# Scores against the block summaries: two 64-query tiles in one TensorE product

## The chip, the cores and the metric

The kernel runs on one core of one Trainium2 chip. The metric is the device time of one execution in microseconds; lower is better. Of the kernel before there are three timed runs, with a median of 678.67 us, and one profiled execution, whose trace all views here are taken from.

## What is computed

The reference is an attention whose output goes through one feed-forward layer. Each query sees the keys less than 16 positions away and, beside them, one summary of each block of 32 keys (the maximum of the block's keys, the mean of its values). Batch is 4, heads 8, sequence 768, head dimension 64; the feed-forward layer has width 512 and inner width 2048.

```python
k_sum = k.reshape(B, H, nb, block, D).max(axis=3)      # block 32, nb 24
v_sum = v.reshape(B, H, nb, block, D).mean(axis=3)
scores_l = scale * np.matmul(q, k.transpose(0, 1, 3, 2))
mask_l = np.abs(pos[:, None] - pos[None, :]) < window  # window 16
scores_s = scale * np.einsum('bhsd,bhnd->bhsn', q, k_sum) + np.log(block)
a = softmax(concatenate([where(mask_l, scores_l, -1e9), scores_s]))
x = matmul(a, concatenate([v, v_sum]))                 # heads side by side: 3072 x 512
h = x @ w_in
return (h * np.cos(h)) @ w_out
```

## The kernel before

**Groups.** The attention is cut into 32 groups: eight blocks of 384 queries (half a sequence each, `blk` 0 to 7) by four pairs of heads (`a`, `b`, `c`, `d`). A group holds six tiles of 64 queries for two heads. A tile of 64 queries needs a window of 96 keys (64 and 16 on either side) and the 24 summaries, so 120 scores a query and head.

**Scores.** The transposed queries of both heads lie in `qd` (128 partitions: head dimension of the first head, then of the second; 384 columns, one a query), the transposed keys in `kd` of the head pair, with the 24 summaries behind the keys from column `KW` on. The scores of head `hh` are built in one PSUM bank, `self.sp[hh]`: partitions 0 to 63 hold the even tile of a pair (`s` = 0), 64 to 127 the odd one (`s` = 1), and the pairs `c` = 0, 1, 2 lie behind one another, 96 window columns and 24 summary columns each. `scores` (L553 to L566) writes them with four products for each tile: for each head one against the tile's own 96 keys and one against the 24 summaries. Each contracts over 64 partitions (one head) and writes 64 partitions (one tile), so it uses a 64x64 quarter of TensorE's 128x128 array; head and half of the pair choose the quarter. Inputs are fp32, and each product stands in the trace as two passes, each a weight load and a matmul.

In the first eight groups (`masks`) a product with the identity (L549) has put the mask into the bank, and the score products add to it; in the other 24 VectorE adds the mask as it takes the scores out (`scale`, L573). Then follow maximum, subtraction, exponential, sum and normalization (VectorE, GpSimd, ScalarE), a transposition of the probabilities (L619, or in later groups through DRAM), the products with the values (`values`, L663) and a split of the result into a high and a low part.

**The feed-forward layer.** Weights and activations are split into high and low parts (fp32r), and each product is made of three. A step is one slice of 128 of the inner width for one block of 384 rows: `up` (L707, 12 products of 384 columns), cosine by ScalarE and VectorE (L717 to L732), a split again (L343, L349), `down` (L751, 9 products of 512 columns). There are 128 steps, so 1536 products on L707 and 1152 on L751.

**Order.** One list written out by hand (`ORDER`) gives the order in which every engine's instructions are issued; nothing is rescheduled. A token such as `d7.sc.2.5` is one call: here the scores of group d of block 7 into banks 2 and 5. The scores of all groups but the first eight stand between steps of the feed-forward layer, most directly between an `up` (L707) or `down` (L751) and the next.

The part that issues the score products, before:

```python
for t in range(U):                       # six tiles
    c, s = divmod(t, 2)
    for hh in range(2):
        for lo, n, key in ((0, W, k0), (W, NB, KW)):
            nc.tensor.matmul(out=self.sp[hh][s * QT : (s + 1) * QT, c, lo : lo + n], ...)
```

Of the kernel before, what the change touches and what calls it, by code (L numbers as in the profile page):

```python
# [176 lines left out]
def tile_kernel(  # L177
# [20 lines left out]
    nc = tc.nc  # L198

    B, H, S, D = q.shape  # L200
    NT, DM = out.shape
    DF = w_in.shape[1]
    P = 128
    QT = 64
    W = QT + 2 * WINDOW
    NB = S // BLOCK
    SQ = 32
    NK = W + NB
    NPAIR = H // 2
    TB = S // 2  # L210
    U = TB // QT
    NG = NPAIR
    QC = TB // P
# [69 lines left out]
    for hh in range(2):  # L283
        rows = mask[hh * QT : (hh + 1) * QT, :, 0:W]

        nc.gpsimd.affine_select(
            out=rows, in_=rows, pattern=[[0, QC + 1], [1, W]], compare_op=ALU.is_ge,
# [3 lines left out]
            out=rows, in_=rows, pattern=[[0, QC + 1], [-1, W]], compare_op=ALU.is_ge,  # L291
# [7 lines left out]
    KW = WINDOW + S + WINDOW  # L299
# [122 lines left out]
    class Group:  # L422
# [130 lines left out]
        def scores(self, *two):  # L553
            if not self.masks:
                self.score_banks(two)
            for t in range(U):
                c, s = divmod(t, 2)
                k0 = self.base + t * QT
                for hh in range(2):
                    rows = slice(hh * D, (hh + 1) * D)  # L560
                    for lo, n, key in ((0, W, k0), (W, NB, KW)):
                        nc.tensor.matmul(  # L562
                            out=self.sp[hh][s * QT : (s + 1) * QT, c, lo : lo + n],
                            lhsT=self.qd[rows, t * QT : (t + 1) * QT], rhs=self.kd[rows, key : key + n],
                            start=not self.masks, stop=not self.masks or (c == QC - 1 and lo == W),
                        )  # L566

        def scale(self, hh, eng):
            out = self.sc.rearrange("p (c h) n -> p c h n", h=2)[:, :, hh, :]
# [260 lines left out]
    class Summaries:  # L830
# [16 lines left out]
        def sum(self, eng):  # L847
# [24 lines left out]
            lo="low_part", dn="down", fe="fetch", ad="add", ta="take", st="store",  # L872
# [39 lines left out]
```

## Time and profile before

| | |
|---|---|
| timed runs | 677.88, 678.67, 681.73 us (median 678.67) |
| profiled execution | 679.78 us, of which the span from first to last instruction is 678.0 |
| TensorE busy (matmuls) | 641.4 us, 95% of the span |
| TensorE weight loads | 564.8 us (most beside matmuls) |
| VectorE, ScalarE, GpSimd busy | 391.1, 411.6, 295.4 us |
| score products (L562) | 768 products, 1536 passes, from 12.5 to 547.4 us |
| mean granted TensorE clock | 0.984 |

How to read it: in the profile PE is TensorE's matmuls, PEld its weight loads, DVE is VectorE, ACT ScalarE, POOL GpSimd, SP the queue that issues transfers. A line such as L562 is a line of the kernel before; `banks` is all of PSUM, `kd` keys, `qd` queries (in the first groups also in a buffer named `late`), `xh` and `xl` the parts of the layer's input, `gh` and `gl` those of the gate, `w` the weights. "64\*64" behind an operation is rows\*columns of the array in use, "64x96" partitions and columns of the operand. Matmul records end where a model of the pipeline puts their end, so consecutive ones overlap. A row of the table by stage is a stretch, its length, then busy time and instruction count of each engine.

### The profile page before, as it was taken

To read this page: it belongs to the slowest core of one execution; us is meant where nothing else is said; L and a number is where in the kernel's file an instruction comes from. 1 tells how busy PE (TensorE), PEld (TensorE's weight loads), DVE (VectorE), ACT (ScalarE), POOL (GpSimd) and SP (SyncE) were. 2 spreads that over 40 slices of the span, in tenths; PEclk is the share of its full clock that TensorE was granted. 3 is DMA by queue.
4 is the path that set the end of the run, shared out by engine and by line. 5 is a ranking of instruction groups with operands and counts; after the bars stand their busy time and mean duration, and the time that the engine had idled before them with its cause. 6 is when DMAs were issued, how large, how long until landed. Compare 5 with 4: busy or idle time off the path is not lost.

```text
span 678.0 us, 13401 instructions
## 1 busy us (share of the span) xinstructions
PE 641.4 (95%) x5180; PEld 564.8 (83%) x5180; DVE 391.1 (58%) x642; ACT 411.6 (61%) x720; POOL 295.4 (44%) x312
## 2 busy tenths in 40 slices
PE   6439989999999999999999999999999999999996
PEld 4327768888888888888898888898898889899895
DVE  3889799987553467426775764248484652232221
ACT  3557887758765467646765765447666565455443
POOL 3665778655432355333444554414353442122221
PEclk9959999999999999999999999999999999999999
DMA  9797924442322323434545453433253440001001
GB/s 221 212 252 195 321 83 159 149 110 59 87 51 54 88 78 112 117 89 95 111 123 129 118 166 95 94 53 89 75 148 90 107 124 29 23 0 47 1 0 47
DMA packets 158543, 71.17 MB, mean 105 GB/s; under 512 B 129552, under 2 KB 147344, under 8 KB 158480
## 3 DMA queue, kind: packets, MB, share of 16 engines
q1 hardware_dynamic: 158480, 70.32, 39.0%
q8 instruction: 41, 0.67, 0.4%
q14 instruction: 22, 0.18, 0.1%
HBM read 52.99 MB, written 14.94 MB: 100 GB/s over the span
## 4 chain that ended last, share of the span: by engine, by line
PE 86%; DMA 5%; DVE 3%; ACT 2%; SPq 2%; POOL 2%; issue 1%; POOLq 0%; ACTq 0%; DVEq 0%
PE banks L707 38%; PE banks L751 37%; PE banks L562 4%; DMA late<-in_moe_w_out_dram 4%; PE banks L663 4%; SPq L449 1%; PE banks L549 1%; PE banks L619 1%; POOL w L349 1%; DMA kn<-in_v_dram 1%; DVE banks L400 1%; DVE banks L392 1%; DVE stage L386 1%; PE banks L495 0%; PE banks L508 0%
## 5 line engine op out<-in xcount | busy, mean ns | idle before, releaser
L707 PE MATMUL banks<-xh,w 128*128 128x384 f32 x1024 | 281.9, 338 | 0.0
L751 PE MATMUL banks<-w,gh 128*128 128x512 f32 x768 | 242.6, 397 | 0.0
L349 POOL TENSOR_TENSOR gl<-t,gh 128x384 fp32r<-128x384 f32 x123 | 126.0, 1026 | 251.1 <-ACT gh L343 185.7
L707 PEld LDWEIGHTS banks<-xh,w 128*128 128x128 f32 x1024 | 186.9, 188 | 4.7 <-DVE xl L349 0.2
L707 PE MATMUL banks<-xl,w 128*128 128x384 f32 x512 | 171.8, 336 | 0.0
L751 PEld LDWEIGHTS banks<-w,gh 128*128 128x128 f32 x768 | 140.2, 188 | 25.6 <-ACT gh L343 0.2
L751 PE MATMUL banks<-w,gl 128*128 128x512 f32 x384 | 151.7, 395 | 0.6 <-POOL gl L349 0.4
L720 DVE SCALAR_TENSOR_TENSOR t<-t,banks 128x384 f32<-128x384 int32 x128 | 70.3, 549 | 127.6 <-ACT t L717 127.4
L717 ACT ACTIVATE t<-banks 128x384 int32<-128x384 f32 x128 | 62.4, 487 | 104.0 <-PE banks L707 100.3
L732 DVE SCALAR_TENSOR_TENSOR t<-t,banks 128x384 f32<-128x384 f32 x128 | 70.2, 549 | 75.5 <-ACT t L728 75.0
L707 PEld LDWEIGHTS banks<-xl,w 128*128 128x128 f32 x512 | 96.1, 188 | 3.8
L725 ACT ACTIVATE t<-t 128x384 f32<-128x384 f32 x128 | 67.2, 525 | 44.1 <-DVE t L720 43.8
L343 ACT CAST gh<-t 128x384 fp32r<-128x384 f32 x115 | 58.8, 512 | 55.1 <-DVE t L732 50.9
L751 PEld LDWEIGHTS banks<-w,gl 128*128 128x128 f32 x384 | 72.0, 188 | 18.0 <-POOL gl L349 2.4
L728 ACT ACTIVATE t<-t 128x384 f32<-128x384 f32 x128 | 67.2, 525 | 3.6
L586 POOL TENSOR_TENSOR sc<-sc,m 128x720 f32<-128x720 f32 x28 | 40.7, 1453 | 41.8 <-DVE m L581 39.0
L610 POOL TENSOR_TENSOR sc<-sc,r 128x720 f32<-128x720 f32 x28 | 38.9, 1392 | 38.5 <-DVE r L607 33.7
L349 POOL TENSOR_TENSOR w<-stage,w 128x1024 fp32r<-128x1024 f32 x15 | 36.6, 2440 | 18.2 <-ACT w L343 17.5
L562 PEld LDWEIGHTS banks<-kd,qd 64*64 64x64 f32 x1344 | 27.5, 132 | 7.9 <-issue 5.5
L602 DVE TENSOR_REDUCE r<-sc 128x6 f32<-128x726 f32 x28 | 25.2, 902 | 14.5 <-ACT sc L599 14.4
L725 ACT ACT_TABLE_LOAD x24 | 30.8, 1283 | 0.4
L562 PE MATMUL banks<-kd,qd 64*64 64x96 f32 (+1 forms) x1344 | 30.4, 231 | 0.1
(97 smaller groups left out, 577.4 us busy)
## 6 DMA issues: line engine op xcount, KB each, us to landing
late<-in_moe_w_in_dram SPq DMA_DIRECT2D x16, 512.0 KB
late<-in_moe_w_out_dram SPq DMA_DIRECT2D x16, 512.0 KB
pd<-stage SPq DMA_DIRECT2D x20, 384.0 KB
vn<-in_v_dram SPq DMA_DIRECT2D x52, 120.0 KB
out_dram<-stage SPq DMA_DIRECT2D x24, 256.0 KB
pt<-pd SPq DMA_DIRECT2D x60, 96.0 KB
kn<-in_v_dram SPq DMA_DIRECT2D x24, 192.0 KB
qn<-in_q_dram SPq DMA_DIRECT2D x80, 48.0 KB
```

The source lines that it names most:

```text
L343: eng.copy(out=out, in_=in_)
L349: eng.tensor_tensor(out=lo, in0=src, in1=hi.bitcast(F32), op=ALU.subtract)
L562: nc.tensor.matmul(out=self.sp[hh][s * QT : (s + 1) * QT, c, lo : lo + n], lhsT=self.qd[rows, t * QT : (t + 1) * QT], rhs=self.kd[rows, ke ...
L586: nc.gpsimd.tensor_tensor(out=self.sc, in0=self.sc, in1=self.m.unsqueeze(2).broadcast_to([P, U, NK]), op=ALU.subtract)
L610: nc.gpsimd.tensor_tensor(out=self.sc, in0=self.sc, in1=self.r.unsqueeze(2).broadcast_to([P, U, NK]), op=ALU.mult)
L707: nc.tensor.matmul(out=self.h, lhsT=w_of(name, self.f)[:, c * P : (c + 1) * P], rhs=x_of(self.blk, part, c), start=n == 0, stop=n == last,)
L717: nc.scalar.activation(out=self.t.bitcast(I32), in_=self.h, func=AF.Copy, scale=1.0 / TWO_PI)
L720: nc.vector.scalar_tensor_tensor(out=self.t, in0=self.t.bitcast(I32), scalar=-TWO_PI, in1=self.h, op0=ALU.mult, op1=ALU.add)
L725: nc.scalar.activation(out=self.t, in_=self.t, func=AF.Sin, scale=0.5)
L728: nc.scalar.activation(out=self.t, in_=self.t, func=AF.Square, scale=math.sqrt(2.0))
L732: nc.vector.scalar_tensor_tensor(out=self.t, in0=self.t, scalar=-1.0, in1=self.h, op0=ALU.add, op1=ALU.mult)
L751: nc.tensor.matmul(out=self.acc[i], lhsT=g[:, i * P : (i + 1) * P], rhs=w_of(name, self.f), start=self.first and n == 0, stop=self.last an ...
```

## The change

The products against the 24 summaries are the same for every query of a head, so two neighbouring tiles can share one. For each pair `c` the changed kernel first issues the four window products (two tiles by two heads, 64x64 each), and then for each head one product of all 128 queries of the pair with the summaries: it contracts over 64 partitions and writes 128, so it uses a 64x128 half of the array. A group has 12 + 6 = 18 products in place of 24. What is computed, where it is put, and the order of calls are the same.

```diff
-            for t in range(U):
-                c, s = divmod(t, 2)
-                k0 = self.base + t * QT
+            for c in range(QC):
+
+                for s, hh in itertools.product(range(2), range(2)):
+                    rows, k0 = slice(hh * D, (hh + 1) * D), self.base + (2 * c + s) * QT
+                    nc.tensor.matmul(
+                        out=self.sp[hh][s * QT : (s + 1) * QT, c, :W],
+                        lhsT=self.qd[rows, (2 * c + s) * QT : (2 * c + s + 1) * QT], rhs=self.kd[rows, k0 : k0 + W],
+                        start=not self.masks, stop=not self.masks,
+                    )
                 for hh in range(2):
                     rows = slice(hh * D, (hh + 1) * D)
-                    for lo, n, key in ((0, W, k0), (W, NB, KW)):
-                        nc.tensor.matmul(
-                            out=self.sp[hh][s * QT : (s + 1) * QT, c, lo : lo + n],
-                            lhsT=self.qd[rows, t * QT : (t + 1) * QT], rhs=self.kd[rows, key : key + n],
-                            start=not self.masks, stop=not self.masks or (c == QC - 1 and lo == W),
-                        )
+                    nc.tensor.matmul(
+                        out=self.sp[hh][:, c, W:NK],
+                        lhsT=self.qd[rows, c * P : (c + 1) * P], rhs=self.kd[rows, KW : KW + NB],
+                        start=not self.masks, stop=not self.masks or c == QC - 1,
+                    )
```

The order of instructions shows what this does on TensorE; rows that read alike one after the other are counted (x4). The first place is the last score group of the program, between a `down` (L751) and an `up`. Here is its beginning before, where `64x96` is a window product and `64x24` a summary product (partitions of the weights' columns written, by columns):

```order
L751 MATMUL banks<-w_394,gh 128x512 x2
L751 MATMUL banks<-w_394,gl 128x512
L562 MATMUL banks<-kd_102,qd 64x96
L562 MATMUL banks<-kd_102,qd 64x24
L562 MATMUL banks<-kd_102,qd 64x96
L562 MATMUL banks<-kd_102,qd 64x24
```

The last two rows go on in turn to 24 products. The same group whole in the changed kernel, where L561 is the window product, L568 the summary product, L757 `down` and L713 `up`:

```order
L757 MATMUL banks<-w_370,gl 128x512
L561 MATMUL banks<-kd_102,qd 64x96 x4
L568 MATMUL banks<-kd_102,qd 128x24 x2
L561 MATMUL banks<-kd_102,qd 64x96 x4
L568 MATMUL banks<-kd_102,qd 128x24 x2
L561 MATMUL banks<-kd_102,qd 64x96 x4
L568 MATMUL banks<-kd_102,qd 128x24 x2
L713 MATMUL banks<-xh_6_5151,w_680 128x384
```

Window and summary products no longer take turns one by one; they stand in six runs of four and two, and every second run writes 128 partitions.

The second place is in the start of the program, on TensorE as well, where the scores of the second block's first group follow the mask product (L549, after the change L550) and a product with the values (L663, L669). Before:

```order
L495 MATMUL banks<-ident,late_128 128x128 x3
L663 MATMUL banks<-pt,x_1_136 64x64 x12
L549 MATMUL banks<-mask,ident 128x360 x2
L562 MATMUL banks<-kd_99,qd 64x96
L562 MATMUL banks<-kd_99,qd 64x24
```

The changed kernel at the same place:

```order
L496 MATMUL banks<-ident,late_128 128x128 x3
L669 MATMUL banks<-pt,x_1_136 64x64 x12
L550 MATMUL banks<-mask,ident 128x360 x2
L561 MATMUL banks<-kd_99,qd 64x96 x4
L568 MATMUL banks<-kd_99,qd 128x24 x2
```

What stands ahead of the scores and behind them is the same; only the score products themselves are regrouped. On VectorE, ScalarE, GpSimd and the transfer queue no instruction changes its place.

More of the change, by code (lines that the diff above doesn't have):

```diff
@@ L1 @@
+import itertools
 import math
```

## The prediction

> **What bounds the kernel now.** I read the page first: its engine line, its slices and its chain, which follows the work that ended last back to the start.
>
> ```profile
> span 678.0 us, 13401 instructions
> PE 641.4 (95%) x5180; PEld 564.8 (83%) x5180; DVE 391.1 (58%) x642; ACT 411.6 (61%) x720; POOL 295.4 (44%) x312
> ...
> PE   6439989999999999999999999999999999999996
> ...
> PE 86%; DMA 5%; DVE 3%; ACT 2%; SPq 2%; POOL 2%; issue 1%; POOLq 0%; ACTq 0%; DVEq 0%
> PE banks L707 38%; PE banks L751 37%; PE banks L562 4%; DMA late<-in_moe_w_out_dram 4%; PE banks L663 4%; SPq L449 1%; PE banks L549 1%; PE banks L619 1%; POOL w L349 1%; DMA kn<-in_v_dram 1%; DVE banks L400 1%; DVE banks L392 1%; DVE stage L386 1%; PE banks L495 0%; PE banks L508 0%
> ```
>
> TensorE carries 86% of the chain, and the score line L562, which the change rewrites, is 4% of it. From the fourth slice on TensorE has no hole. The table by stage makes that sharp, first for all work, then for L562 alone in three stretches:
>
> ```profile
> 147.00:550.00 403.00, 403.00 (x3458) 358.37 (x3457) 234.28 (x423) 251.40 (x436) 170.59 (x177) 1.00 0.40 99
> ```
> ```profile
> 0.00:147.00 147.00, 8.70 (x384) 7.86 (x384) 0.93 0.67 190
> ```
> ```profile
> 147.00:550.00 403.00, 26.09 (x1152) 23.58 (x1152) 1.00 0.40 99
> ```
> ```profile
> 46.00:70.00 24.00, 4.35 (x192) 3.93 (x192) 0.86 0.78 201
> ```
>
> The first two numbers after a stretch are its length and TensorE's busy time: 403.00 of 403.00 us between 147 and 550, at a granted clock of 1.00. There a microsecond more on TensorE is a microsecond more at the end. The counts in brackets place the groups: 24 products in two passes each are 48 instructions a group, so 1152 are 24 of the 32 groups, all inside the full stretch. Eight lie ahead of 147 us, four of them (192) between 46 and 70 us. The chain in order of time tells which of the eight count:
>
> ```profile
> 53.72 1.02 PE banks L562 x36
> ...
> 56.75 1.02 PE banks L562 x36
> ...
> 61.07 1.02 PE banks L562 x36
> ...
> 68.67 1.03 PE banks L562 x36
> ...
> 69.73 0.82 ACT late L343 x2
> ...
> 74.25 9.28 DMA late<-in_moe_w_out_dram
> ...
> 109.88 1.88 PE banks L751 x7
> ```
>
> All four of that stretch are on it; what follows them is ScalarE and a transfer, and TensorE takes the chain again at 109.88. The first four groups (12 to 27 us) are not on it. So 24 groups count for certain, four by this chain, four not.
>
> **What a group costs now.** The busy time of L562 in one group's stretch, from its first instruction to the next line's:
>
> ```profile
> 546.49:547.51 1.02, 1.01 (x48) 0.98 (x48) 1.00 0.00 0
> ```
>
> It is 1.02 us for 48 passes, 0.34 us for each of the three pairs of tiles c, though the passes' own durations (264 and 198 ns on average) add up to eleven times that:
>
> ```profile
> L562 PE MATMUL banks<-kd,qd 64*64 64x96 f32 x672 | 28.2, 264 | 0.1
> L562 PE MATMUL banks<-kd,qd 64*64 64x24 f32 x672 | 24.4, 198 | 0.0
> ```
>
> So the four quarters of the array (two heads by two halves of the query pair) work side by side. The timeline of TensorE shows it, and what a change of the array's shape costs. Columns are start, length, line, rows*columns of the array in use, and count:
>
> ```profile
> 546.17 0.40 PE L751 MATMUL banks<-w,gl 128*128 128x512 f32 x1
> 546.50 1.09 PE L562 MATMUL banks<-kd,qd 64*64 64x96 f32 x48
> 547.51 0.45 PE L707 MATMUL banks<-xh,w 128*128 128x384 f32 x1
> 547.80 0.34 PE L707 MATMUL banks<-xl,w 128*128 128x384 f32 x1
> 547.97 0.51 PE L707 MATMUL banks<-xh,w 128*128 128x384 f32 x2
> ```
>
> Between two products of one shape the next starts 0.17 us before the end of the one ahead (547.80 + 0.34 against 547.97). Where the shape changes it starts only 0.07 us before: 546.17 + 0.40 against 546.50, and 546.50 + 1.09 against 547.51. The pipeline is let run out. The same stands between two shapes that are both parts of the array, here L562 and L663:
>
> ```profile
> 490.47 0.64 PE L562 MATMUL banks<-kd,qd 64*64 64x96 f32 x27
> 491.04 0.92 PE L663 MATMUL banks<-pt,vn 120*64 120x64 f32 x24
> 491.89 0.41 PE L562 MATMUL banks<-kd,qd 64*64 64x96 f32 x8
> ```
>
> 490.47 + 0.64 against 491.04, 491.04 + 0.92 against 491.89: 0.07 us again, both ways. The Trainium skill, page "TensorEngine Tiling (Array Packing)", Tiling Modes, Key Properties, says it as a rule: changing the tiling mode, not merely the tile, drains TensorE. The five changes seen above agree, but a change between 64x64 and 64x128 stands in no row of before.
>
> **The change part by part.** Removed: six products of a 64x64 quarter with 24 columns, twelve passes a group. Added: the 24-column products of a pair run on a 64x128 half. Moved: the four 96-column products of a pair now stand together, then the two wide ones, so a group goes 64x64, 64x128, 64x64, 64x128, 64x64, 64x128. That is five changes of shape inside a group where there were none. Nothing moves on any other engine; the wait of the first summary product for VectorE's summaries stays with the first wide one, now behind four products instead of one, and costs nothing where TensorE is late anyway.
>
> *The narrow phase.* Its eight passes stand in before at the burst's start, four first and four second passes (from start of the burst to the end of the eighth):
>
> ```profile
> 546.50 0.33 PE L562 MATMUL banks<-kd,qd 64*64 64x96 f32 x4
> ```
> ```profile
> 546.63 0.28 PE L562 MATMUL banks<-kd,qd 64*64 64x96 f32 x4
> ```
>
> They end at 546.63 + 0.28 = 546.91; with the 0.07 the next shape could start at 546.84. So the narrow phase costs 0.34 us, already the whole of what a pair costs now.
>
> *The wide phase.* What a weight load of 128 columns costs when nothing hides it is seen after a change of shape: L707's first product takes 0.45 us where the next takes 0.34, so 0.11 us, and the second load starts 0.11 after the first:
>
> ```profile
> 547.51 0.19 PEld L707 LDWEIGHTS banks<-xh,w 128*128 128x128 f32 x1
> 547.62 0.19 PEld L707 LDWEIGHTS banks<-xl,w 128*128 128x128 f32 x1
> ```
>
> For the 64-column load the same comparison has the means of the four first and the four second passes, 293 and 242 ns, so 0.05 us:
>
> ```profile
> L562 PE MATMUL banks<-kd,qd 64*64 64x96 f32 x4 | 0.3, 293 | 0.0
> ```
> ```profile
> L562 PE MATMUL banks<-kd,qd 64*64 64x96 f32 x4 | 0.3, 242 | 0.0
> ```
>
> A 24-column pass lasts at least 182 ns, so from its start to the next shape 0.18 - 0.07 = 0.11 us:
>
> ```profile
> L562 PE MATMUL banks<-kd,qd x1344: 182/228/294, 12.5 to 547.4; 64*64 64x96 f32 x96, 64*64 64x24 f32 x96
> ```
>
> Two passes on each half, the halves side by side 0.01 us apart (four of the quarters' first passes start within 0.33 - 0.29 = 0.04 us): 0.11 + 0.11 for the loads, which a 24-column pass is too short to hide, 0.01 for the second half, 0.11 to run out: 0.34 us.
>
> *Sum.* A pair 0.34 + 0.34 = 0.68, a group 2.04 in place of 1.02: +1.02 us. The ends for the one unknown duration, the wide load: 0.11 by L707, or 0.05 as in the 64-column row, where the wide phase is 0.05 + 0.05 + 0.01 + 0.11 = 0.22 and a group costs 3 x 0.56 - 1.02 = +0.66 us. I take 0.11, since it is the row with as many columns. A gain in this term is excluded, since the narrow phase alone uses up the pair's 0.34.
>
> *Groups.* The 24 in the full stretch give +24.5 us. Of the four early ones I count two, half: the chain holds them, but a transfer and ScalarE work follow, and a path behind the longest can swallow part. 26 x 1.02 = +26.5; bounds 24 and, if even the first four counted, 32 (+32.6). The scores reach VectorE a microsecond later in each group; nothing in 147 to 550 made TensorE wait, so this has slack at least as long as TensorE is the late one.
>
> The profiled execution took 679.78 us with a span of 678.0; span + 26.5 = 704.5. The runs' median, 678.67, lies 1.1 below that execution: 678.67 + 26.5 = **705.2 us**.
>
> **The rivals.**
>
> *The count of passes decides (not slower).* If TensorE is limited by how many passes it starts, and 64x64 to 64x128 is no change that drains, 36 passes at 1.02/48 = 21 ns cost 0.77 us: -0.25 a group, 26 groups -6.6, 672.1 us. It decides once the two phases of a pair together stay under 0.34 us. For it: nothing in the trace shows this pair of shapes. Against it: the four first passes start 0.01 us apart, so starts are not what is short. The Trainium skill, "TensorEngine Tiling (Array Packing)", Performance Considerations, Instruction Overhead, gives about 60 cycles to each matmul however few its columns; by an estimate from it (25 ns at the 2.4 GHz that "TensorE: Matmul & The Clock Gate", Part 1, gives the array, 12 passes) a group gains 0.3 us and the kernel about 8. The 0.01 us between starts on different quarters speaks against the rule here. Chance 0.04.
>
> *No drain, and the load alone decides.* A quarter then pays 0.08 us for a 96-column pass (first to second pass, 546.50 to 546.63, less the 0.05 of the load) and one load for each 24-column pass, since the pass is shorter than the load. Two and two of these are 0.26 with loads of 0.05, near the 0.34 measured. If wide loads take 0.05 as well, a pair costs what it costs now: 678.7, chance 0.03. With 0.11 it is 0.06 x 2 more a pair, 0.36 a group, +9.4, 688.1, chance 0.03. For it: no row of before shows this pair of shapes; against it, the five changes above.
>
> *Drain one way only.* If the wide load may start under the last narrow passes, a pair saves their run-out, 0.28 - 0.07 - 0.08 = 0.13, and most of the first load, 0.08: 0.68 - 0.21 = 0.47, a group +0.39, 26 groups +10, 688.8. For it: quarters do run ahead of one another. Against it: all five changes of shape seen drain. Chance 0.05.
>
> *The two halves' wide loads go one after the other.* Then two more loads, 0.22 a pair, 0.66 a group: +1.68, 26 groups +43.7, 722.4. Against it: loads of quarters start with the passes, 0.01 apart. Chance 0.03.
>
> **How the numbers follow.** The forecast holds 0.82. Its own ends are 24 groups at 0.66 (+15.8, 694.5) and 32 at 1.02 (+32.6, 711.3); the runs of before reach 3.1 us above their median, which I add at both ends: 691.4 to 714.4, rounded 691 to 714. The rivals outside hold 0.18, so the range need not reach to them. About 0.5% (3.4 us) is what a measurement of this kernel can tell from no change. Faster by more: the count, 0.04. Within: 0.03. Slower: 0.82 + 0.03 + 0.05 + 0.03 = 0.93.
>
> **What would show it.** Right: a group's stretch from first score product to the next line near 2.04 us in place of 1.02; six phases in it, each starting 0.07 us before the modelled end of the phase ahead; wide passes with first durations some 0.11 us above later ones; TensorE still without a hole from 147 us on, with L707 and L751 unchanged in duration and the end moved by the sum over 24 groups and a part of the early ones. Wrong: wide passes that start before the narrow ones have run out (a group near 1.4 us), a group under 1.02, or a group of 2 us with an end that moved by much less than 24 of them, which would mean that TensorE had slack between 147 and 550 us that its busy time hides.

## The result, and the profile after

The changed kernel takes 705.17 us (median of four runs, 703.22 to 707.34), the kernel before in the same measurement 679.94 (677.88 to 681.73). The ratio is 1.0384 with a 95% interval of 1.0348 to 1.0419: slower, by some 26 us. The profiled execution of the changed kernel took 703.22 us with a span of 701.4, 23.4 more than the span before.

The page of the changed kernel, with its engine line, TensorE's slices and the chain; L561 and L568 are the window and the summary products, L713 and L757 the layer's `up` and `down`:

```profile
span 701.4 us, 12633 instructions
PE 670.3 (96%) x4796; PEld 581.3 (83%) x4796; DVE 390.8 (56%) x642; ACT 411.9 (59%) x720; POOL 294.0 (42%) x312
...
PE   6559899999999999999999999999999999999996
...
PE banks L713 37%; PE banks L757 36%; PE banks L568 4%; PE banks L561 4%; DMA late<-in_moe_w_out_dram 3%; PE banks L669 3%; DMA late<-in_v_dram 1%; SPq L450 1%; PE banks L625 1%; PE banks L550 1%; POOL w L350 1%; DMA x<-vs 1%; DVE stage L409 0%; PE banks L496 0%; PE banks L509 0%
```

There are 384 fewer passes (4796 in place of 5180) and 28.9 us more TensorE time. On the chain the scores have grown from 4% to 4% + 4%; no other engine has more to do.

The table by stage from 147 us to just behind the last score group (its last three numbers are granted clock, DMA share and GB/s):

```profile
147.00:572.00 425.00, 425.00 (x3163) 370.27 (x3162) 234.70 (x422) 251.91 (x435) 169.46 (x176) 1.00 0.37 94
```

TensorE is without a hole here as before, at a granted clock of 1.00. The last score group ends at 570.93 us where it ended at 547.51, 23.4 us later.

The timeline of TensorE around the last score group (start, length, line, rows\*columns of the array, count):

```profile
568.62 0.40 PE L757 MATMUL banks<-w,gl 128*128 128x512 f32 x1
568.95 0.40 PE L561 MATMUL banks<-kd,qd 64*64 64x96 f32 x8
569.27 0.41 PE L568 MATMUL banks<-kd,qd 64*128 64x24 f32 x4
569.61 0.40 PE L561 MATMUL banks<-kd,qd 64*64 64x96 f32 x8
569.94 0.41 PE L568 MATMUL banks<-kd,qd 64*128 64x24 f32 x4
570.27 0.40 PE L561 MATMUL banks<-kd,qd 64*64 64x96 f32 x8
570.60 0.41 PE L568 MATMUL banks<-kd,qd 64*128 64x24 f32 x4
570.93 0.45 PE L713 MATMUL banks<-xh,w 128*128 128x384 f32 x1
```

The group lasts from 568.95 to 570.93, 1.98 us where it was 1.02. Six phases are seen, narrow ones of 0.33 and wide ones of 0.33 to 0.34 us, and each starts 0.07 to 0.08 us before the modelled end of the one ahead: 568.95 + 0.40 against 569.27, 569.27 + 0.41 against 569.61. So 24 groups cost 24 x 0.96 = 23 us more, which is within 0.4 us the difference of the two spans.

The weight loads in the same stretch:

```profile
569.27 0.30 PEld L568 LDWEIGHTS banks<-kd,qd 64*128 64x128 f32 x4
569.61 0.21 PEld L561 LDWEIGHTS banks<-kd,qd 64*64 64x64 f32 x8
```

Four wide loads keep the load path for 0.30 us of a phase of 0.34. A phase is little but loading and running out.

In the start stage the chain leads to the point from which TensorE carries it again. Before it read 109.88; the changed kernel has:

```profile
110.01 1.88 PE banks L757 x7
```

In this pair of executions the first eight groups moved that point by only 0.13 us.

### The profile page after: what moved, and what is told of

It is laid out like the page before. It is cut to its first block, busy times and chain, and to the rows that moved or that the text cites. A ratio compares the mean times of both kernels' runs of the same rounds, so it can differ in the third digit from the quotient of the medians.

```text
span 701.4 us, 12633 instructions
## 1 busy us (share of the span) xinstructions
PE 670.3 (96%) x4796; PEld 581.3 (83%) x4796; DVE 390.8 (56%) x642; ACT 411.9 (59%) x720; POOL 294.0 (42%) x312
## 4 chain that ended last, share of the span: by engine, by line
PE 86%; DMA 5%; ACT 2%; DVE 2%; SPq 2%; POOL 1%; issue 1%; POOLq 0%; ACTq 0%; DVEq 0%
PE banks L713 37%; PE banks L757 36%; PE banks L568 4%; PE banks L561 4%; DMA late<-in_moe_w_out_dram 3%; PE banks L669 3%; DMA late<-in_v_dram 1%; SPq L450 1%; PE banks L625 1%; PE banks L550 1%; POOL w L350 1%; DMA x<-vs 1%; DVE stage L409 0%; PE banks L496 0%; PE banks L509 0%
## 5 line engine op out<-in xcount | busy, mean ns | idle before, releaser
L713 PE MATMUL banks<-xh,w 128*128 128x384 f32 x1024 | 281.9, 339 | 0.0
L757 PE MATMUL banks<-w,gh 128*128 128x512 f32 x768 | 242.5, 397 | 0.0
L713 PEld LDWEIGHTS banks<-xh,w 128*128 128x128 f32 x1024 | 186.9, 188 | 4.4
L713 PE MATMUL banks<-xl,w 128*128 128x384 f32 x512 | 171.8, 336 | 0.0
L757 PEld LDWEIGHTS banks<-w,gh 128*128 128x128 f32 x768 | 140.2, 188 | 25.7 <-ACT gh L344 0.2
L757 PE MATMUL banks<-w,gl 128*128 128x512 f32 x384 | 151.9, 395 | 2.0 <-POOL gl L350 1.9
L713 PEld LDWEIGHTS banks<-xl,w 128*128 128x128 f32 x512 | 96.2, 188 | 3.8
L757 PEld LDWEIGHTS banks<-w,gl 128*128 128x128 f32 x384 | 72.0, 188 | 19.3 <-POOL gl L350 3.8
L579 DVE SCALAR_TENSOR_TENSOR sc<-banks,mask 128x360 f32<-128x360 f32 x48 | 23.5, 523 | 26.0 <-PE banks L568 26.0
L568 PE MATMUL banks<-kd,qd 64*128 64x24 f32 x336 | 34.0, 276 | 0.0
L568 PEld LDWEIGHTS banks<-kd,qd 64*128 64x128 f32 x336 | 25.3, 184 | 9.9
L561 PE MATMUL banks<-kd,qd 64*64 64x96 f32 x672 | 33.3, 268 | 0.2 <-ACT qd L502 0.2
```

The lines of the kernel that those rows point to most:

```text
L561: nc.tensor.matmul(out=self.sp[hh][s * QT : (s + 1) * QT, c, :W], lhsT=self.qd[rows, (2 * c + s) * QT : (2 * c + s + 1) * QT], rhs=self.kd ...
L568: nc.tensor.matmul(out=self.sp[hh][:, c, W:NK], lhsT=self.qd[rows, c * P : (c + 1) * P], rhs=self.kd[rows, KW : KW + NB], start=not self.m ...
L713: nc.tensor.matmul(out=self.h, lhsT=w_of(name, self.f)[:, c * P : (c + 1) * P], rhs=x_of(self.blk, part, c), start=n == 0, stop=n == last,)
L757: nc.tensor.matmul(out=self.acc[i], lhsT=g[:, i * P : (i + 1) * P], rhs=w_of(name, self.f), start=self.first and n == 0, stop=self.last an ...
```

## The experiments

Theory: each change of the array's shape lets the pipeline run out and leaves the next weight loads uncovered, and an uncovered wide load costs 0.11 us where a narrow one costs 0.05. Rivals: only the load's width costs; the regrouping by itself costs; the count of passes decides; the early groups carry much of the loss. A difference in us below is the ratio less one, times the median of the kernel before in the same measurement: 679.08 us for the first eight groups, windows first, the change's order with narrow products and one load, 679.47 us for the other runs.

**The first eight groups alone.**

The changed loops stand under a condition, the old ones under its other branch.

```diff
+            if self.masks:
+                for c in range(QC):
...
+            else:
+                for t in range(U):
...
```

> The change in the first eight groups alone (those whose mask is put into PSUM by a product); the other 24 as before. Theory (the end moves by what TensorE does in its full stretch; ahead of 147 us transfers and other engines decide): each of the eight costs 0.97 us more on TensorE, but the end moves by 0 to 2 us. Rival (the chain of before is right for the four groups between 46 and 70 us, so they count in full): +3.9 us; all eight in full: +7.7 us.

Measured: 682.13 us against 679.08, ratio 1.0044 (1.0018 to 1.0070), +3.0 us with +1.2 to +4.8. The middle lies above the theory's 0 to 2; +2 and +3.9 are both inside the interval. The chain in its profile comes to TensorE at

```profile
112.55 1.88 PE banks L770 x7
```

2.7 us later than before (L770 is `down` there). It leaves TensorE once more, which waits 0.41 us for GpSimd ahead of 146.85, and the first of the later 24 groups starts at 151.46 where before had it at 147.87. The changed kernel, whose first eight groups are the same as here, had it at 148.01; and three runs below whose first eight groups are as before had it between 147.23 and 149.06. So one profile can't tell how much of the early groups arrives: that start moves by some us from run to run. By the times, eight in full (+7.7) is excluded, and which of the four count is not settled.

**The other 24 alone.** The two branches are exchanged.

> The counterpart of the run on the first eight groups: the change in the 24 groups between 147 and 550 us alone, the first eight as before. Theory (in the full stretch every microsecond of TensorE counts): 24 x (1.98 - 1.02) = +23.2 us over before, 3.4%, and together with the first eight's 3 us the change's whole. Rival (TensorE had slack there, and the early groups make up more than their own run showed): +18 us or less.

Measured: 702.45 us against 679.47, ratio 1.0338 (1.0306 to 1.0369), +23.0 us. TensorE is without a hole again:

```profile
147.00:570.00 423.00, 423.00 (x3152) 368.33 (x3150) 233.03 (x419) 251.23 (x433) 168.04 (x176) 1.00 0.37 93
```

The full stretch passes on all of it. 1.0044 x 1.0338 = 1.0383, the change's 1.0384: the two parts make the whole.

**Windows first: one change of shape in place of five.** A second loop over `c` stands ahead of the wide products.

```diff
             for c in range(QC):
                 for s, hh in itertools.product(range(2), range(2)):
...
+            for c in range(QC):
                 for hh in range(2):
                     rows = slice(hh * D, (hh + 1) * D)
...
```

> The 18 products of the change, but all 12 window products first and then all 6 wide ones: one change of shape inside a group in place of five. Theory (each change of shape lets the pipeline run out, and wide loads of 0.11 us are not hidden): window phase 0.15 + 4 x 0.08 + 0.17 = 0.64 us, wide phase 6 x 0.11 + 0.01 + 0.11 = 0.78, a group 1.42 us where before has 1.02 and the change 1.98; about +9.6 us over before with 24 groups, some 689. Rival (the wide loads alone are the cost, changes of shape are free): as much as the change, +23 to +25 us. Rival (the count of passes decides): 36 passes as in the change, so no difference to the change.

Measured: 690.47 us, ratio 1.0175 (1.0141 to 1.0208), +11.9 us. Its timeline in the last group:

```profile
556.67 0.73 PE L561 MATMUL banks<-kd,qd 64*64 64x96 f32 x24
557.32 0.85 PE L569 MATMUL banks<-kd,qd 64*128 64x24 f32 x12
558.11 0.44 PE L714 MATMUL banks<-xh,w 128*128 128x384 f32 x1
```

The windows take 0.65 us, the wide products 0.79, the group 1.44 (expected 1.42). With the same 18 products and the same loads as the change, four changes of shape fewer save 0.54 us a group. That loads alone cost, and that the count of passes decides, both fall. 24 x 0.42 is 10 us; the rest lies within the interval and what the first eight groups add.

**The order of the change with 24 narrow products.** The wide product is split into two of 64 queries; order as in the change.

```diff
-                for hh in range(2):
-                    rows = slice(hh * D, (hh + 1) * D)
+                for s, hh in itertools.product(range(2), range(2)):
+                    rows, t = slice(hh * D, (hh + 1) * D), 2 * c + s
                     nc.tensor.matmul(
-                        out=self.sp[hh][:, c, W:NK],
-                        lhsT=self.qd[rows, c * P : (c + 1) * P], rhs=self.kd[rows, KW : KW + NB],
+                        out=self.sp[hh][s * QT : (s + 1) * QT, c, W:NK],
+                        lhsT=self.qd[rows, t * QT : (t + 1) * QT], rhs=self.kd[rows, KW : KW + NB],
```

> 24 products of 64x64 as before, but in the order of the change: per pair four window products, then four narrow summary products. No change of shape, no wide load. Theory: a group stays at 1.02 us within 0.05, the kernel within 0.5% of before. Rival (grouping by itself breaks the work side by side of the quarters, since short products then stand together): a group near 1.98 us, the kernel as slow as with the change.

Measured: 677.81 us, ratio 0.9987 (0.9968 to 1.0006): no difference. The last two of the three pairs in its last group:

```profile
545.51 0.37 PE L561 MATMUL banks<-kd,qd 64*64 64x96 f32 x8
545.70 0.26 PE L568 MATMUL banks<-kd,qd 64*64 64x24 f32 x8
545.79 0.37 PE L561 MATMUL banks<-kd,qd 64*64 64x96 f32 x8
545.99 0.26 PE L568 MATMUL banks<-kd,qd 64*64 64x24 f32 x8
546.17 0.44 PE L713 MATMUL banks<-xh,w 128*128 128x384 f32 x1
```

Within one shape the summaries start 0.17 us before the windows' end (545.79 + 0.37 against 545.99) and not 0.07, and two phases take 0.38 with the run-out, not 0.67. Regrouping costs nothing; the group takes 0.97 us. The ends are modelled, but the starts alone say the same: from the windows of one pair to those of the next it is 0.28 us here (545.51 to 545.79), and 0.66 in the changed kernel (568.95 to 569.61).

**Windows first with 24 narrow products.** Both edits at once: the control for the run with windows first.

> 24 products of 64x64: all 12 window products first, then all 12 narrow summary products. The order of the run with windows first, without its wide products and its one change of shape. Theory: windows 0.15 + 4 x 0.08, narrow summaries 0.08 + 5 x 0.05, run-out 0.14: a group 0.96 us, the kernel as before within 0.5%. So of the 1.44 us that windows first and six wide products took, 0.48 are the wide loads and the one change. Rival (long stretches of one kind of product cost something by themselves, in windows first too): a group well over 1.02 us.

Measured: 679.98 us, ratio 1.0009 (0.9988 to 1.0029). In the last group:

```profile
546.62 0.73 PE L561 MATMUL banks<-kd,qd 64*64 64x96 f32 x24
547.16 0.49 PE L569 MATMUL banks<-kd,qd 64*64 64x24 f32 x24
547.59 0.44 PE L714 MATMUL banks<-xh,w 128*128 128x384 f32 x1
```

0.97 us a group (expected 0.96). Twelve narrow summary products take 0.43 us up to the next line, where six wide ones took 0.79, and start 0.11 us earlier. The same sums cost more in half as many products.

**Five changes of shape with narrow loads.** In the 24 later groups, here against the changed kernel, two products a pair contract over 128 partitions, so that their loads have 64 columns.

```diff
-                for hh in range(2):
-                    rows = slice(hh * D, (hh + 1) * D)
+                for s in range(2):
                     nc.tensor.matmul(
-                        out=self.sp[hh][:, c, W:NK],
-                        lhsT=self.qd[rows, c * P : (c + 1) * P], rhs=self.kd[rows, KW : KW + NB],
+                        out=self.sp[s][s * QT : (s + 1) * QT, c, W:NK],
+                        lhsT=self.qd[:, (2 * c + s) * QT : (2 * c + s + 1) * QT], rhs=self.kd[:, KW : KW + NB],
```

> Five changes of shape as in the change, but with 64-column weight loads: in the 24 later groups the summary products contract over both heads' 128 partitions for one tile of 64 queries (128x64), two a pair, so 18 products a group. They write the sum of both heads' scores into half of the summary places and leave the other half unwritten, so these scores are wrong; the first eight groups are as before. Theory (the change's wide phase of 0.33 us is two loads of 0.11 and the run-out): with loads of 0.05 the second phase is 0.05 + 0.05 + 0.01 + 0.11 = 0.22, a group 3 x (0.33 + 0.22) = 1.65 us, 24 groups +15 us over before. Rival (changes of shape are the whole cost, the width of the load none): a group at 1.98 us, +23 us.

Measured: 696.42 us, ratio 1.0252 (1.0216 to 1.0288), +17.1 us. The end of two groups, before a `down` and before products with the values:

```profile
148.39 0.40 PE L574 MATMUL banks<-kd,qd 64*64 64x96 f32 x8
148.71 0.30 PE L580 MATMUL banks<-kd,qd 128*64 128x24 f32 x4
148.95 0.73 PE L769 MATMUL banks<-w,gh 128*128 128x512 f32 x2
```

```profile
271.60 0.30 PE L580 MATMUL banks<-kd,qd 128*64 128x24 f32 x4
271.74 0.48 PE L681 MATMUL banks<-pt,vn 120*64 120x64 f32 x9
```

The second phase takes 0.24 us here (148.71 to 148.95) and 0.23 in the two pairs ahead of it, where the wide one took 0.34: the two loads are about 0.11 shorter together. A group is 1.67 us. So of the change's loss of 0.96 a group, 0.31 is the width of the loads; 0.65 is left with narrow ones. The second piece is the plainest sign of the drain: the products with the values (L681) use the same 64 columns and 120 of the same 128 rows, and they start 0.16 us before the modelled end of the summaries, not 0.07.

**Twice the changes of shape.** One head at a time in the 24 later groups: two windows, one wide product.

```diff
-            for c in range(QC):
-
-                for s, hh in itertools.product(range(2), range(2)):
...
-                for hh in range(2):
...
+                for c, hh in itertools.product(range(QC), range(2)):
                     rows = slice(hh * D, (hh + 1) * D)
+                    for s in range(2):
+                        k0 = self.base + (2 * c + s) * QT
...
```

> The same 18 products as the change in the 24 later groups, but one head at a time: two window products, the head's wide product, and so on; 11 changes of shape inside a group in place of five. The first eight groups are as before. Theory (each phase pays its first load, its last pass and the run-out anew): a window phase 0.13 + 0.01 + 0.17 = 0.31, a wide phase 0.13 + 0.20 = 0.33, a group 6 x 0.64 = 3.8 us, +67 us over before. Rival (a change of shape costs a fixed 0.14 us, as (1.98 - 1.44) / 4 in the run with windows first): 1.98 + 6 x 0.14 = 2.8 us, +43 us. Rival (changes of shape are free): a group at 1.98 us, +23 us.

Measured: 786.5 us, ratio 1.1557 (1.1502 to 1.1613), +105.8 us: more than any of the three gave. The group itself is as the theory had it:

```profile
149.06 0.38 PE L574 MATMUL banks<-kd,qd 64*64 64x96 f32 x4
149.38 0.40 PE L579 MATMUL banks<-kd,qd 64*128 64x24 f32 x2
149.71 0.38 PE L574 MATMUL banks<-kd,qd 64*64 64x96 f32 x4
```

A pair of phases from 149.06 to 149.71 is 0.65 us although it holds half the products. Twelve phases take 3.85 us in the groups that run at full clock throughout, 3.89 in this one. The fixed price (2.8 us) falls: a change costs its whole short phase. 24 x (3.85 - 1.02) = 68 us, as expected; the other 38 are for the most part the clock. The table by stage, first for one group, then for the stretch right behind it, then for the whole full stretch:

```profile
149.06:152.80 3.74, 3.74 (x37) 2.86 (x36) 0.56 (x1) 2.13 (x4) 2.15 (x3) 1.00 0.70 194
153.00:156.40 3.40, 3.40 (x9) 2.67 (x9) 3.31 (x6) 1.05 (x2) 0.89 (x1) 0.53 0.00 0
...
147.00:650.00 503.00, 503.00 (x3175) 431.72 (x3174) 235.44 (x424) 252.87 (x437) 172.56 (x177) 0.93 0.32 81
```

Behind the group the granted clock is 0.53 for 3.4 us, though TensorE was busy by its records all the time. Over the full stretch it is 0.93, and 0.07 x 503 = 35 us is about what the group's own sum leaves open. The mean clock of its four runs is 0.925 to 0.938, that of the 16 runs of the kernel before beside them 0.976 to 0.987.

**One load for window and summary.** Twelve products of 120 columns, in all 32 groups.

```diff
-                    for lo, n, key in ((0, W, k0), (W, NB, KW)):
+                    for lo, n, key in ((0, NK, k0),):
...
```

> Twelve products of 64x64 with 120 columns a group, one for each tile and head: the tile's window and the 24 columns behind it, which are further keys and not the summaries; so the summary scores are left out and other numbers stand in their place, everything behind goes on unchanged. Theory (a 24-column pass costs its 0.05 us weight load and not its columns): a quarter has six passes of 0.10, a group 0.15 + 4 x 0.10 + 0.02 + 0.19 = 0.77 us, -0.25 a group, 24 groups -6 us, some 0.9% faster than before. Rival (columns streamed decide): the columns are the same 120, so no difference to before.

Measured: 674.5 us, ratio 0.9932 (0.9908 to 0.9955), -4.6 us, the expected -6 within the interval. The last group:

```profile
542.29 0.85 PE L562 MATMUL banks<-kd,qd 64*64 64x120 f32 x24
543.07 0.45 PE L707 MATMUL banks<-xh,w 128*128 128x384 f32 x1
```

0.78 us in place of 1.02, with as many columns. What the short product cost here is its load: to save a load within the shape was worth 0.24 us a group, to make the load wider was a loss. A kernel that computes the reference this way needs the 24 summaries between every tile's keys, twelve copies in each of four key buffers, 264 columns more or 4.1 KB a partition, beside weights that take 128 KB. No run shows whether they fit, and such a kernel was not tried on the chip.

## Why the prediction was right

**What bounds it.** Right: TensorE's full stretch hands on every microsecond; the 24 groups alone give +23.0 us. That TensorE has no hole "from the fourth slice on" passes over the 8 in the sixth slice (it is busy for 13.93 of the 17 us from 85 to 102), but the sum rests on 147 to 550 us, where it is right.

**Narrow phase** 0.34: measured 0.33. **Wide phase** 0.34, with the wide load at 0.11 and not at 0.05: measured 0.34, and with a 64-column load in its place 0.23, as the lower end of the range had it (0.22). In the trace a half's second load starts 0.11 us after its first, a quarter's 0.05. One sign that the prediction named did not come: the first wide passes last 287 ns and the second ones 266, 0.02 us apart and not 0.11, since the second ones wait for a wide load as well; the phase's sum holds. **Group** +1.02: measured +0.96. The small rest is in the starts: where the four quarters' first passes stood 0.013 us apart before, they stand 0.007 apart now.

**Drain between 64x64 and 64x128**, inferred from other pairs of shapes (the prediction speaks of five changes; its rows show four): shown. The starts lie 0.07 to 0.08 us before the ends ahead at every one of the five new changes, and the runs with one change (1.44 us), five (1.98) and eleven (3.85) leave no room for a free change or a fixed price. The Trainium skill, page "TensorEngine Tiling (Array Packing)", Tiling Modes, Key Properties, says that a change of tiling mode drains TensorE, and one of tile does not: the trace agrees in both halves, 0.07 us where the shape changes, 0.16 us where L681, with the same columns and no split of the rows, follows L580.

**Groups that count.** 24 for certain was right. Two of the four early ones (+2.0 us) was a choice between bounds; alone they gave +3.0, with +1.2 to +4.8, which does not tell two from four. With +23.0 that makes 26.0, where the prediction had 26.5. That the time came out within 0.1 us of 705.2 is luck: a group cost 0.06 us less than forecast, the early groups gave perhaps 1 us more, and the kernel before took 679.94 us beside the changed one and not 678.67.

**The rivals.** The count of passes and the columns streamed both fell. No drain would have given a group of 1.02 or 1.38 us, drain one way 1.41, wide loads one after the other 2.70; the group is 1.98. The about 60 cycles for each matmul that the Trainium skill, page "TensorEngine Tiling (Array Packing)", Performance Considerations, Instruction Overhead, names would have made fewer passes faster; here 48 passes in 0.97 us, 20 ns each across four quarters, beat 36 in 1.98.

## What to carry to other kernels

Before merging small products, look at what each costs in its place: here a 24-column product cost its quarter a weight load of 0.05 us, which four quarters paid side by side. The merged one cost its half a load of 0.11 us, plus a change of the array's shape on either side. Count the changes of shape in TensorE's order, not the products, and put products of one shape together. Where a stage has no hole on TensorE, the change of one group's time times the number of groups is the change of the kernel's time, as long as the granted clock stays: with eleven changes of shape in a group it did not.

## What was not expected

With eleven changes of shape in a group, TensorE's granted clock fell to about half for some microseconds after a group (0.53 from 153.0 to 156.4 us) and to 0.93 over 503 us. The trace has sixteen such stretches between 147 and 650 us, of 3.4 to 10.2 us each. They cost about a third of the loss, without any idle time in TensorE's records. With five changes it stayed at 1.00. The Trainium skill, "TensorE: Matmul & The Clock Gate", Part 1, section "A second HAM failure mode: psum-queue depth-cycling", tells of a clock that swings because TensorE is idle for moments between groups of products; this run has the swing, and the moments would be the drains, which its records do not show as idle. That the drains set it off is not shown: no run varied them apart from the length of the group, which is 3.85 us here and 1.98 in the changed kernel.
